# Windowed attention, a gated block and a token and channel mixer on one core: another plan for the first stage, with norms on GpSimd

## The chip, the core and the metric

The kernel runs on one core of one Trainium2 chip. The metric is the device time of one execution in microseconds (us). TensorE (PE in the profile) multiplies matrices into PSUM; VectorE (DVE), ScalarE (ACT) and GpSimd (POOL) work on tiles of 128 partitions; SyncE (SP) issues the DMAs that move data between HBM and SBUF.

## The reference

Three parts follow each other, all in float32 (the weights of the second and third part come as float64 words):

```python
# attention: 4 batches, 8 heads, 576 tokens, head size 64, each token sees itself and 63 before it
scores = where(0 <= rel < 64, q @ k.T / 8, -1e9)
attn = exp(scores - max); attn = attn / (sum(attn) + 1e-9); x = attn @ v
# gated block
h = relu(x @ w_in); u, v = h[..., :512], h[..., 512:]
v_n = (v - mean(v)) / sqrt(var(v) + 1e-6)
x = (u * (w_spatial @ v_n + b_spatial)) @ w_out
# mixer
u = x + (relu(x.T @ w_tok1) @ w_tok2).T
out = u + relu(u @ w_ch1) @ w_ch2
```

## The kernel before

The work up to about 224 us is recorded by a planner, `plan()`; behind it the rest (the product with `w_out`, the mixer) stands in written order and is not touched.

The planner's class `Steps` holds steps with a name, an engine, a rank, a duration, the steps that must be done first and the buffers they take and give back. It plays time forward and records on each engine the possible step that can start first, by rank among equals. The order of each engine's instructions is thereby fixed before the kernel runs; each engine then works its list in order and waits where an input is late.

Attention goes in 18 turns (two passes over batch pairs, nine turns each) of 128 tokens and 8 heads. The steps of turn n, where g is 0 or 1 for a half of four heads:

- `S`: the score products on PE (`scores`), 16 pairs of matmuls into two PSUM banks. For turns below `MASK_PE` = 6 the mask is added on PE too, by one bf16 product of 512 columns for each bank (L278).
- `M`: the row maximum on DVE. For turns below 6 one reduction and one small multiplication (L294, L301); for later ones the mask is added and the maximum found in one custom instruction for each head, from PSUM into the SBUF tile `pb` (L297).
- `X`: four exponentials on ACT with their sums (L306), from PSUM for turns below 6, from `pb` for later ones.
- `N`: on DVE, 1e-9 is added to the sums, the reciprocal taken, and `pb` multiplied by it (L314, L315, L316).
- `T`: four transposes on PE (L488); `C`: the copy of these from PSUM to the tile `PT`, on ACT (L489).
- `V`: the product with the values (L324). The first `PAIRS` = 4 turns have a `V` of their own, later ones go in pairs. `xh`, `xl`: the result split into two rounded parts, on ACT and DVE (L538, L543).

Of these parts come the products of the gated block on PE: `v` (one for each turn, 12 matmuls of 512 columns), then on ACT `R`, on DVE `bn` (L372, L373), on POOL `rs` (L375, L376), on DVE `ts` (L378), and `hi`, `lo`; `u` (four for every third turn, 12 matmuls of 384 columns; evicted by `E`); and `s` (the product over the tokens, 14 matmuls of 288 columns), with `G` on DVE (L406), which multiplies into `U`.

`w_in` is 8 tiles of 512 KB, four for `v` and four for `u`. Each is loaded as float64 words into a piece of `U` and turned into float32 there: `wd` on ACT (into a PSUM bank), `wo` on DVE (two instructions on that bank, L439, L440), `wh` on ACT and `wl` on DVE (L445). `ws` are the tiles of `w_spatial`, split on ACT and DVE. `c2_work` prepares `w_c2` in the same manner in the gaps, with four sums on POOL, and sends it to HBM (`scr`). `wo_work` prepares `w_out`, behind the step `gate`, which waits for the last `xl`; its loads share two buffers (`craw`). SP's first loads stand in one line, in the order in which the tuple before `score` names them.

Of the kernel before, what the change touches and what calls it, by code (L numbers as in the profile page):

```python
# [20 lines left out]
P = 128  # L21
# [4 lines left out]
MASK_PE = 6  # L26
# [3 lines left out]
PAIRS = 4  # L30
# [8 lines left out]
class Steps:  # L39
# [5 lines left out]
    def __init__(self, **room):  # L45
        self.room = {k: [0.0] * n for k, n in room.items()}
        self.clock, self.done, self.open, self.lines = {}, {}, [], {}
        self.pad, self.queue, self.lands = 0, 0.0, [0.0] * 8
# [5 lines left out]
    def start(self, step):  # L54
        name, eng, rank, us, fn, after, take, give, hold, kb = step
        at = self.clock.get(eng, 0.0)
        for a in after:
            if a not in self.done:
                return None
            at = max(at, self.done[a] + self.LAG)  # L60
        for r in set(take):
            free, n = sorted(self.room[r]), take.count(r)
            if len(free) < n:
                return None
            at = max(at, free[n - 1] + self.LAG)
        return max(at, self.lands[-8 + (kb > 520)]) if kb else at

    def run(self):
        while True:
# [10 lines left out]
            gap = at - self.clock.get(eng, 0.0)  # L80
            self.pad = int((gap - 0.5) / 0.3) if PAD and eng == "PE" and gap > 0.8 and at < PAD else 0
# [16 lines left out]
def tile_kernel(ctx, tc, qT, kT, kE, v, w_in, wsT, b_sp, w_out, w_t1, w_t2, w_c1, w_c2, outT):  # L98
# [361 lines left out]
    def plan():  # L460
# [11 lines left out]
        def attend(n):  # L472
# [8 lines left out]
            def turned(g):  # L481
# [7 lines left out]
                copies[n, g] = lambda: nc.scalar.copy(out=PT[0][:, 4 * g:4 * g + 4, :], in_=pt)  # L489

            for g in range(2):
                S.add(("M", n, g), "DVE", 1 + n / 100, 0.95, lambda g=g: smax(n, g), after=[("S", n)], give=free * (n >= MASK_PE))
                S.add(("X", n, g), "ACT", 2 + n / 100, 1.65, lambda g=g: sexp(n, g), after=[("M", n, g)], give=free * (n < MASK_PE), hold=1.54)
                S.add(("N", n, g), "DVE", 1 + n / 100, 1.15, lambda g=g: snorm(n, g), after=[("X", n, g)], hold=1.05)
                S.add(("T", n, g), "PE", 1 + n / 100, 0.65, lambda g=g: turned(g), after=[("N", n, g)], take=free + ["PT"] * (g == 0), give=["pb"] * g, line=("T", n), hold=0.45)
                S.add(("C", n, g), "ACT", 1, 0.6, lambda g=g: copies.pop((n, g))(), after=[("T", n, g)], give=free, hold=0.49)
# [7 lines left out]
        def score(n, after, line):  # L504
            S.add(("S", n), "PE", 0, 1.2 + 0.6 * (n < MASK_PE), lambda: scores(n), after=after + [("Lq", n), "ident"],
                  take=[] if after else ["sp", "sp", "pb"], give=["qk"], hold=1.0 + 0.6 * (n < MASK_PE), line=line)

        def block(ns):
# [36 lines left out]
        def v_work(p, i):  # L545
# [15 lines left out]
            S.add(("v", n), "PE", 10, 2.9, product, after=[("xl", n)] + [("wl", "v", k) for k in range(4)], take=["mm"], hold=2.75, line="work")  # L561
            S.add(("R", n), "ACT", 1.5, 0.6, relu, after=[("v", n)], take=["vf"], give=["mm"], hold=0.49)
            S.add(("bn", n), "DVE", 2, 0.9, part, after=[("R", n)])
            S.add(("rs", n), "POOL", 0, 1.0, part, after=[("bn", n)])
            S.add(("ts", n), "DVE", 2, 0.56, part, after=[("rs", n)])
            S.add(("hi", n), "ACT", 4, 0.6 if i else 2.2, part, after=[("ts", n)])
            S.add(("lo", n), "DVE", 3, 0.7 if i else 1.3, part, after=[("hi", n)], give=["vf"])

        def u_work(p, c, ft):
            g = {}  # L570

            def product():
# [3 lines left out]
            S.add(("u", p, c, ft), "PE", 10, 2.25, product, after=[("xl", 9 * p + 3 * c + k) for k in range(3)] + [("wl", "u", ft)],  # L576
                  take=["mm"], give=["XT"] * (ft == 3), hold=2.09, line="work")
            S.add(("E", p, c, ft), "ACT", 1.5, 0.5 if c == 2 else 0.72, lambda: uv_u_out(p, c, ft, g["ps"]), after=[("u", p, c, ft)], give=["mm"])

        def s_work(b, d, c0):  # L580
# [8 lines left out]
            S.add(("s", b, d, c0), "PE", 10, 2.0, product, after=tiles + [("ws", k, c0) for k in range(6)], take=["mm"], hold=1.86, line="work")  # L589
            S.add(("G", b, d, c0), "DVE", 0.5, 0.47, lambda: spatial_out(b, d, c0, g["ps"]),  # L590
                  after=[("s", b, d, c0)] + [("E", p, c, d) for c in range(2 + b % 2)], give=["mm"], hold=0.4)

        def w_load(kind, k):
            it = (wv_part if kind == "v" else wu_part)(k)
# [3 lines left out]

            S.add(("wL", kind, k), "SP", 0, 0, part, hold=0.47, kb=512, line="SP")
            S.add(("wd", kind, k), "ACT", 1.8 if kind == "v" else 2.5, 0.7, part, after=[("wL", kind, k)], take=["mm"], hold=0.6)  # L600
            S.add(("wo", kind, k), "DVE", 0.8 if kind == "v" else 2.5, 1.25, part, after=[("wd", kind, k)])
            S.add(("wh", kind, k), "ACT", 1.8 if kind == "v" else 2.5, 0.6, part, after=[("wo", kind, k)], hold=0.49)
            S.add(("wl", kind, k), "DVE", 0.8 if kind == "v" else 2.5, 0.7, part, after=[("wh", kind, k)], give=["mm"], hold=0.6)

        def ws_load(k, c):
# [8 lines left out]
            S.add(("wh", k, c), "ACT", 3, 0.45, part, after=[("Lw", k, c)], hold=0.35)  # L614
            S.add(("ws", k, c), "DVE", 2.5, 0.45, part, after=[("wh", k, c)], give=["raw"], hold=0.38)
# [41 lines left out]
        def c2_work(j):  # L657

            rank = 6 + j
# [51 lines left out]
        for fn, *a in ((load_queries, 0), (w_load, "v", 0), (load_queries, 1), (w_load, "v", 1), (load_values, 0), (w_load, "v", 2), (w_load, "v", 3),  # L711
                       (load_queries, 2), (load_values, 1), (w_load, "u", 0), (load_queries, 3), (w_load, "u", 1), (w_load, "u", 2), (w_load, "u", 3)):
# [597 lines left out]
```

## Time and profile before

| | us |
|---|---|
| median of 3 runs (620.10 to 621.08) | 620.14 |
| the profiled execution | 621.39 |
| its span, first to last instruction | 619.5 |
| PE busy in the span | 600.2 (97%) |
| DVE busy | 472.6 (76%) |
| ACT busy | 352.7 (57%) |
| POOL busy | 114.7 (19%) |

The profiled execution is 1.25 us longer than the median, of which 1.9 us lie outside its span. PE's waits sum to some 16 us over the whole span; about 11 us of the first 50 show PE without work. The rows are stretches of a timeline (start, duration, engine, line, operation, tiles, count, and in brackets the idle time before and what ended it), groups of instructions, and busy time in windows.

### The profile page before, as it was taken

What the parts mean: (1) busy time and instruction counts of PE and PEld (TensorE: products, weight loads), DVE (VectorE), ACT (ScalarE), POOL (GpSimd) and SP (SyncE); (2) the same over time, 40 slices, a digit from 0 to 9 for tenths busy, and PEclk for the clock granted to TensorE, in tenths of its full rate; (3) what the DMA queues carried; (4) which work ended last, traced back from release to release, by engine and by line L of the source; (5) the groups of instructions that cost most, each with busy time, mean ns of one, the idle gap of its engine ahead of it and who ended that gap; (6) DMA issues with size and microseconds to landing.
All of it is one profiled execution on the core that took longest, in us unless ns stands there. A gap on an engine that the chain in (4) does not pass through costs nothing.

```text
span 619.5 us, 12149 instructions
## 1 busy us (share of the span) xinstructions
PE 600.2 (97%) x4396; PEld 560.6 (90%) x4396; DVE 472.6 (76%) x1066; ACT 352.7 (57%) x889; POOL 114.7 (19%) x145
## 2 busy tenths in 40 slices
PE   4999999999999989999999999999999999999997
PEld 2678899889988989788988999999999999999997
DVE  5998878968888836586278778888875989866982
ACT  5996786766777532674344454546443557544540
POOL 3000202302422200041025212140011140011320
PEclk8899999999999999999999999999999999999999
DMA  8956356866565652415200524665534674444752
GB/s 325 342 187 188 124 198 228 262 225 223 203 203 180 229 179 69 137 57 167 84 34 35 170 69 169 221 224 168 184 126 173 230 234 159 153 137 170 237 197 77
DMA packets 49812, 108.05 MB, mean 174 GB/s; under 512 B 4948, under 2 KB 17496, under 8 KB 49752
## 3 DMA queue, kind: packets, MB, share of 16 engines
q1 hardware_dynamic: 49752, 107.27, 51.2%
q8 instruction: 35, 0.57, 0.4%
q14 instruction: 25, 0.20, 0.1%
HBM read 86.81 MB, written 20.45 MB: 173 GB/s over the span
## 4 chain that ended last, share of the span: by engine, by line
PE 62%; DVE 4%; DMA 4%; ACT 2%; issue 1%; POOL 0%; ACTq 0%
PE A L1167 19%; PE mm L183 13%; PE mm L955 12%; PE A L955 9%; PE A L183 6%; DMA scr<-raw 3%; PE A L873 1%; DMA craw<-in_w_out 1%; PE A L1251 1%; DVE pb L297 1%; DVE raw L689 0%; ACT raw L686 0%; DVE pb L316 0%; DVE st L372 0%; DVE hid L949 0%
## 5 line engine op out<-in xcount | busy, mean ns | idle before, releaser
L1167 PE MATMUL A<-room,w 128*128 128x384 f32 x720 | 131.1, 335 | 0.7 <-DVE U L1203 0.7
L1167 PEld LDWEIGHTS A<-room,w 128*128 128x128 f32 x720 | 125.1, 188 | 2.1 <-DVE U L1203 1.0
L1161 ACT CAST room<-hid 128x384 fp32r<-128x384 f32 x120 | 61.3, 513 | 48.9 <-PE A L1167 37.5
L1162 DVE TENSOR_TENSOR room<-hid,room 128x384 fp32r<-128x384 f32 x120 | 71.9, 625 | 13.9 <-ACT room L1161 12.2
L949 POOL TENSOR_TENSOR hid<-hid 128x384 f32<-128x384 f32 x36 | 44.2, 1239 | 202.8 <-DVE hid L949 160.0
L183 PE MATMUL mm<-ws,room 128*128 128x288 f32 x416 | 61.0, 297 | 1.6 <-DVE U L406 1.5
L183 PEld LDWEIGHTS mm<-ws,room 128*128 128x128 f32 x416 | 56.7, 188 | 2.6 <-DVE U L406 2.1
L980 ACT ACTIVATE hid<-hid 128x384 f32<-128x384 f32 x54 | 28.1, 525 | 42.4 <-DVE hid L983 42.4
L983 DVE TENSOR_TENSOR hid<-A,hid 128x384 f32<-128x384 f32 x54 | 29.5, 554 | 24.7 <-PE A L955 18.4
L306 ACT ACTIVATE pb<-pb,nm 128x128 f32<-128x128 f32 x96 | 37.2, 392 | 2.8 <-DVE nm L297 2.8
L955 PE MATMUL mm<-room,sh 128*128 128x384 f32 x144 | 37.2, 334 | 0.0
L183 PE MATMUL mm<-xh,wi_h 128*128 128x384 f32 x96 | 33.2, 346 | 0.0
L183 PE MATMUL mm<-xh,wi_l 128*128 128x384 f32 x96 | 32.2, 336 | 0.0
L183 PE MATMUL mm<-xl,wi_h 128*128 128x384 f32 x96 | 32.2, 335 | 0.0
L1192 DVE TENSOR_TENSOR U<-A,U 128x384 f32<-128x384 f32 x42 | 21.9, 551 | 11.1 <-PE A L1167 6.5
L183 PE MATMUL mm<-gh,wo_h 128*128 128x512 f32 (+1 forms) x80 | 30.2, 378 | 0.0
L183 PE MATMUL mm<-gl,wo_h 128*128 128x512 f32 (+1 forms) x80 | 29.6, 370 | 0.2 <-DVE gl L855 0.2
L813 POOL TENSOR_TENSOR k<-k 128x256 f32<-128x256 f32 x12 | 9.7, 832 | 107.1 <-ACT gh L854 59.4
L183 PE MATMUL mm<-gh,wo_l 128*128 128x512 f32 (+1 forms) x80 | 29.5, 369 | 0.0
L855 DVE TENSOR_TENSOR gl<-U,gh 128x512 fp32r<-128x512 f32 (+1 forms) x20 | 13.3, 667 | 21.1 <-ACT gh L854 21.0
L488 PE MATMUL sp<-ident,pb 128*128 128x128 f32 x144 | 21.7, 284 | 7.0 <-DVE pb L316 3.0
L170 ACT CAST sh<-k 128x1024 fp32r<-128x1024 f32 x18 | 18.9, 1050 | 15.7 <-PE mm L955 5.9
(181 smaller groups left out, 1546.0 us busy)
## 6 DMA issues: line engine op xcount, KB each, us to landing
w<-scr SPq DMA_DIRECT2D x63, 512.0 KB, 4.1
scr<-raw SPq DMA_DIRECT2D x48, 256.0 KB, 3.5
k<-sums SPq DMA_DIRECT2D x18, 512.0 KB, 3.8
kk<-in_kT SPq DMA_DIRECT2D x16, 384.0 KB, 5.5
craw<-in_w_c SPq DMA_DIRECT2D x24, 256.0 KB, 3.7
qq<-in_qT SPq DMA_DIRECT2D x18, 256.0 KB, 5.5
va<-in_v SPq DMA_DIRECT2D x18, 256.0 KB, 4.4
vb<-in_v SPq DMA_DIRECT2D x18, 256.0 KB, 4.6
```

Of the source, the lines that this page charges most:

```text
L170: nc.scalar.copy(out=hi, in_=x)
L183: nc.tensor.matmul(o, a, c, start=(i == 0), stop=(i == n - 1))
L306: nc.scalar.activation(out=pb[:, h, :], in_=scs[g][:, h - 4 * g, :] if mk is None else pb[:, h, :], func=AF.Exp, scale=SCALE if mk is None ...
L488: nc.tensor.transpose(pt[:, h, :], pb[:, 4 * g + h, :], ident)
L949: eng.tensor_tensor(out=out, in0=a, in1=b, op=ALU.subtract)
L955: nc.tensor.matmul(o, a, m, start=first and i == 0, stop=i == len(todo) - 1, skip_group_check=True)
L980: nc.scalar.activation(out=o, in_=src, func=AF.Relu)
L983: nc.vector.tensor_tensor(out=o, in0=a, in1=b, op=ALU.add)
L1161: nc.scalar.copy(out=oh, in_=blk[j])
L1162: nc.vector.tensor_tensor(out=ol, in0=blk[j], in1=f(oh), op=ALU.subtract)
L1167: nc.tensor.matmul(acc[d], a, m, start=(first and j == 0 and i == 0), stop=(last and j == NJ - 1 and i == 2), skip_group_check=True)
L1192: nc.vector.tensor_tensor(out=at, in0=src, in1=at, op=ALU.add)
```

## The change

The planner gets new numbers: a table of ranks, a table `SLACK` of extra time that it adds behind inputs by the kind of step, a cost for PE's change from one kind of product to another, and new durations. Beside that:

- `MASK_PE` = 0: no mask on PE; all turns use the custom instruction on DVE and take their exponentials from `pb`. The score banks come free behind `M` then.
- The norm is cut in two steps: `I` (the sum's addition and the reciprocal, on DVE) and `N` (the multiplication), which for the turns in `EARLY`, 0 to 9, is on POOL.
- `C` is on DVE for turns 4 to 8.
- `PAIRS` = 6: six turns have a `V` of their own.
- The `u` tiles 0, 2 and 3 of `w_in` are formed in SBUF in their own words (`wu_pool`), without a PSUM bank, and their `wl` is on POOL.
- The first loads stand in another order (`ORDER`).

The diff, cut to its core:

```diff
-MASK_PE = 6
+MASK_PE = 0
-PAIRS = 4
+PAIRS = 6
+EARLY = range(0, 10)
+CD0 = range(4, 9)
+CD1 = range(4, 9)
+PU = (0, 2, 3)
+ORDER = (0, 1, 4, 2, 7, 9, 3, 6, 5, 10, 12, 8, 11, 13)
+RANK = dict(M=3.84, X=22.11, I=-0.06, N=5.51, T=3.58, C=-0.53, ...)
+SLACK = dict(cd=0.68, cs=0, ch=3.08, cl=0.65, oh=1.62, ol=0.52, ...)
...
+        lag = self.LAG + SLACK.get(name[0], 0.0)
         for a in after:
...
-                at = max(at, self.done[a] + self.LAG)
+                at = max(at, self.done[a] + lag)
...
-        nc.vector.tensor_tensor(out=pb[:, hs, :], in0=pb[:, hs, :], in1=rs.unsqueeze(2).to_broadcast([P, w, 128]), op=ALU.mult)
+        yield
+        eng = nc.gpsimd if n in EARLY else nc.vector
+        eng.tensor_tensor(out=pb[:, hs, :], in0=pb[:, hs, :], in1=rs.unsqueeze(2).to_broadcast([P, w, 128]), op=ALU.mult)
...
+    def wu_pool(ft):
+        fs = slice(128 * ft, 128 * ft + 128)
+        raw = U[:, ft, :1024]
+        words = raw.rearrange("p (a c w) -> p a c w", a=4, w=2)
+        x, y, low = words[:, :, :, 1], words.bitcast(I32)[:, :, :, 1], words.bitcast(I32)[:, :, :, 0]
+        hi, lo = wi_h[:, :, fs], wi_l[:, :, fs]
+        nc.sync.dma_start(...)
+        yield
+        down(x, y)
+        yield
+        nc.vector.tensor_scalar(out=y, in0=y, scalar1=3, scalar2=None, op0=ALU.logical_shift_left)
+        nc.vector.scalar_tensor_tensor(out=y, in0=low, scalar=29, in1=y, op0=ALU.logical_shift_right, op1=ALU.bitwise_or)
+        yield
+        nc.scalar.copy(out=hi, in_=x)
+        yield
+        nc.gpsimd.tensor_tensor(out=lo, in0=x, in1=f(hi), op=ALU.subtract)
...
+                    if n in (CD0, CD1)[g]:
+                        nc.vector.tensor_copy(out=out, in_=pt)
+                    else:
+                        nc.scalar.copy(out=out, in_=pt)
```

What the planner makes of it is seen in the lists of the engines. The first place is DVE's list from the end of the first `v` tiles to the first `xl`, before:

```order
L314 TENSOR_SCALAR rs<-sm 128x4
L315 RECIPROCAL rs<-rs 128x4
L316 TENSOR_TENSOR pb<-pb,rs 128x512
L445 TENSOR_TENSOR wi_l<-mm,wi_h 128x512
L439 TENSOR_SCALAR mm<-mm 128x512
L440 SCALAR_TENSOR_TENSOR mm<-U,mm 128x512
L439 TENSOR_SCALAR mm<-mm 128x512
L440 SCALAR_TENSOR_TENSOR mm<-U,mm 128x512
L445 TENSOR_TENSOR wi_l<-mm,wi_h 128x512
L294 TENSOR_REDUCE mx<-sc 128x4
L301 TENSOR_SCALAR nm<-mx 128x4
L543 TENSOR_TENSOR xl<-xo,xh 128x4x128
```

and now, around the first `xl` (L328 and L329 are `I`, L474 and L475 `wo` in SBUF, L455 and L456 `wo` in PSUM, L588 `xl`, L461 `wl`):

```order
L328 TENSOR_SCALAR rs<-sm 128x4
L329 RECIPROCAL rs<-rs 128x4
L474 TENSOR_SCALAR U<-U 128x512
L475 SCALAR_TENSOR_TENSOR U<-U 128x512
L328 TENSOR_SCALAR rs<-sm 128x4
L329 RECIPROCAL rs<-rs 128x4
L455 TENSOR_SCALAR mm<-mm 128x512
L456 SCALAR_TENSOR_TENSOR mm<-U,mm 128x512
L588 TENSOR_TENSOR xl<-xo,xh 128x4x128
L455 TENSOR_SCALAR mm<-mm 128x512
L456 SCALAR_TENSOR_TENSOR mm<-U,mm 128x512
L461 TENSOR_TENSOR wi_l<-mm,wi_h 128x512
```

The large multiplication behind each pair of small instructions is gone from DVE, and `xl` of turn 0 now stands ahead of the `wo` of two of the four `v` tiles, where before it stood behind all four.

The second place is POOL's list behind its set-up. Before, it holds only the two small instructions of `rs` for each `v` product:

```order
L375 TENSOR_SCALAR rstd<-mv 128x1
L376 TENSOR_TENSOR rstd<-rstd,mhalf 128x1
```

and now the multiplications of the norms (L332), the low parts of the three `u` tiles (L479) and `rs` (L391, L392) stand in one line:

```order
L479 TENSOR_TENSOR wi_l<-U,wi_h 128x4x128
L332 TENSOR_TENSOR pb<-pb,rs 128x512 x2
L479 TENSOR_TENSOR wi_l<-U,wi_h 128x4x128
L332 TENSOR_TENSOR pb<-pb,rs 128x512
L479 TENSOR_TENSOR wi_l<-U,wi_h 128x4x128
L391 TENSOR_SCALAR rstd<-mv 128x1
L392 TENSOR_TENSOR rstd<-rstd,mhalf 128x1
L332 TENSOR_TENSOR pb<-pb,rs 128x512
```

Twenty multiplications came to POOL, with the waits of the norms now between those of `rs`.

The third place is SP's list at the end of the plan, where `w_out` is loaded (`craw<-in_w_out`) and the first loads of the mixer's weights begin (`in_w_t`), before:

```order
L621 DMA craw<-in_w_out 128x512 x3
L692 DMA scr<-raw 128x512
L621 DMA craw<-in_w_out 128x512
L692 DMA scr<-raw 128x512 x2
L784 DMA k_3418<-in_w_t 128x2x512
L784 DMA k_3420<-in_w_t 128x2x512
L621 DMA craw<-in_w_out 128x512
L784 DMA k_3422<-in_w_t 64x512
L692 DMA scr<-raw 128x512
L621 DMA craw<-in_w_out 128x512
```

and now:

```order
L670 DMA craw<-in_w_out 128x512 x2
L741 DMA scr<-raw 128x512
L670 DMA craw<-in_w_out 128x512 x2
L741 DMA scr<-raw 128x512 x3
L670 DMA craw<-in_w_out 128x512 x2
L741 DMA scr<-raw 128x512 x2
L670 DMA craw<-in_w_out 128x512 x2
L834 DMA k_3415<-in_w_t 128x2x512
L834 DMA k_3417<-in_w_t 128x2x512
```

The last two loads of `w_out` stood behind loads of the mixer; now all eight stand ahead of them.

## Rows read from the trace of the kernel before

**Rows 1.** Windows: us, then busy time (instructions) of each engine, clock, DMA, GB/s

```profile
10.00:20.00 10.00, 6.62 (x66) 4.80 (x70) 9.72 (x21) 7.84 (x25) 0.00 (x0) 0.53 1.04 391
...
40.00:50.00 10.00, 9.03 (x53) 7.80 (x53) 9.66 (x24) 9.36 (x31) 2.04 (x4) 1.00 0.23 68
```

**Rows 2.** Timeline of PE: scores, `V`, `u`, `v` and transposes

```profile
5.05 1.99 PE L283 MATMUL sc<-kk,qq 64*64 64x128 f32 x32
...
8.68 1.10 PE L283 MATMUL sc<-kk,qq 64*64 64x128 f32 x32 [0.98 <-DMA kk<-in_kT]
...
20.75 1.24 PE L183 MATMUL mm<-wi_h,xh 128*128 128x512 f32 x4
...
53.28 0.34 PE L324 MATMUL mm<-PT,va 128*64 128x64 f32 x4
...
54.36 1.98 PE L283 MATMUL sc<-kk,qq 64*64 64x128 f32 x64
56.27 0.45 PE L183 MATMUL mm<-xh,wi_h 128*128 128x384 f32 x1
...
58.49 1.08 PE L183 MATMUL mm<-wi_h,xh 128*128 128x512 f32 x4
...
61.45 0.63 PE L488 MATMUL sp<-ident,pb 128*128 128x128 f32 x4
61.83 1.18 PE L183 MATMUL mm<-wi_h,xh 128*128 128x512 f32 x4
```

**Rows 3.** DMA of the first 60 us: GB/s in 40 slices of 1.5 us

```profile
GB/s 0 184 416 298 368 412 411 322 403 412 396 404 393 377 382 402 403 398 391 98 103 213 347 276 229 264 164 254 96 0 0 98 0 0 99 81 337 220 260 339
```

**Rows 4.** Timeline of DVE in the first 57 us: norms, weights, statistics, masks

```profile
10.01 0.16 DVE L314 TENSOR_SCALAR rs<-sm 128x4 f32<-128x4 f32 x1
10.21 0.18 DVE L315 RECIPROCAL rs<-rs 128x4 f32<-128x4 f32 x1
10.42 0.69 DVE L316 TENSOR_TENSOR pb<-pb,rs 128x512 f32<-128x512 f32 x1
11.03 0.68 DVE L445 TENSOR_TENSOR wi_l<-mm,wi_h 128x512 fp32r<-128x512 f32 x1
11.63 0.69 DVE L439 TENSOR_SCALAR mm<-mm 128x512 int32<-128x512 int32 x1
...
12.96 0.16 DVE L314 TENSOR_SCALAR rs<-sm 128x4 f32<-128x4 f32 x1
...
28.97 0.69 DVE L372 BATCH_NORM_STATS2 st<-vf 128x6 f32<-128x512 f32 x1
29.69 0.18 DVE L373 BATCH_NORM_AGGREGATE mv<-st 128x2 f32<-128x6 f32 x1
29.79 0.67 DVE L439 TENSOR_SCALAR mm<-mm 128x512 int32<-128x512 int32 x1
...
50.30 1.19 DVE L167 TENSOR_TENSOR ws<-raw,ws 128x288 fp32r<-128x288 f32 x3
...
55.71 0.28 DVE L297 CUSTOM_DVE_ANT_0 pb<-sc,msk 128x128 f32<-128x128 f32 x1
...
56.55 0.29 DVE L297 CUSTOM_DVE_ANT_0 pb<-sc,msk 128x128 f32<-128x128 f32 x1
```

**Rows 5.** POOL's largest group by line: busy us, mean ns, idle time before

```profile
L949 POOL TENSOR_TENSOR hid<-hid 128x384 f32<-128x384 f32 x36 | 44.2, 1239 | 202.8 <-DVE hid L949 160.0 <-DVE room L1162 24.8 <-ACT sh L170 11.9
```

**Rows 6.** One line of DVE, L689: ns min/median/max, first and last start

```profile
L689 DVE TENSOR_TENSOR raw<-cx,raw x24: 415/420/959, 89.5 to 209.0; 128x256 fp32r<-128x256 f32 x24
```

**Rows 7.** Timeline of POOL and DVE at 160 us

```profile
160.49 0.92 POOL L679 TENSOR_TENSOR cy<-cx 128x256 f32<-128x256 f32 x1
160.84 0.85 DVE L378 TENSOR_SCALAR vf<-vf,mv,rstd 128x512 f32<-128x512 f32 x1
```

**Rows 8.** A piece of the chain that ended last: start, us, what

```profile
215.39 7.40 DMA craw<-in_w_out
```

**Rows 9.** Timeline of ACT and PE at the end of the plan

```profile
220.56 0.43 ACT L136 ACTIVATE val<-craw 128x256 f32<-128x256 f32 x1 [4.58 <-DMA craw<-in_w_out]
...
222.19 1.98 PE L183 MATMUL mm<-ws,room 128*128 128x288 f32 x13 [1.48 <-DVE U L406]
```

More of the change, by code (lines that the diff above doesn't have):

```diff
@@ L505, in score @@
             S.add(("S", n), "PE", 0, 1.2 + 0.6 * (n < MASK_PE), lambda: scores(n), after=after + [("Lq", n), "ident"],
-                  take=[] if after else ["sp", "sp", "pb"], give=["qk"], hold=1.0 + 0.6 * (n < MASK_PE), line=line)
+                  take=[] if after else ["sp", "sp", "pb"], give=["qk"], hold=0.98 + 0.6 * (n < MASK_PE), line=line)
         def block(ns):
@@ L530, in block @@
             for m in ns:
-                S.add(("xh", m), "ACT", 0, 0.6, lambda m=m: xhigh(m), after=[("V", m)], hold=0.49)
-                S.add(("xl", m), "DVE", 0, 0.7, lambda m=m: xlow(m), after=[("xh", m)], give=["mm" if m > n else "xo"], hold=0.6)
+                S.add(("xh", m), "ACT", RANK["xh"], 0.6, lambda m=m: xhigh(m), after=[("V", m)], hold=0.49)
+                S.add(("xl", m), "DVE", RANK["xl"], 0.7, lambda m=m: xlow(m), after=[("xh", m)], give=["mm" if m > n else "xo"], hold=0.6)
         def xhigh(n):
@@ L574, in product @@
                 uv_u_mm(p, c, ft, g["ps"])
-            S.add(("u", p, c, ft), "PE", 10, 2.25, product, after=[("xl", 9 * p + 3 * c + k) for k in range(3)] + [("wl", "u", ft)],
-                  take=["mm"], give=["XT"] * (ft == 3), hold=2.09, line="work")
-            S.add(("E", p, c, ft), "ACT", 1.5, 0.5 if c == 2 else 0.72, lambda: uv_u_out(p, c, ft, g["ps"]), after=[("u", p, c, ft)], give=["mm"])
+            S.add(("u", p, c, ft), "PE", 10, 2.3, product, after=[("xl", 9 * p + 3 * c + k) for k in range(3)] + [("wl", "u", ft)],
+                  take=["mm"], give=["XT"] * (ft == 3), hold=2.17, line="work")
+            S.add(("E", p, c, ft), "ACT", RANK["E"], 0.5 if c == 2 else 0.72, lambda: uv_u_out(p, c, ft, g["ps"]), after=[("u", p, c, ft)], give=["mm"])
         def s_work(b, d, c0):
@@ L588, in s_work @@
             tiles = [("lo", 9 * p)] + [("lo", 9 * p + 1 + 4 * (b % 2) + m) for m in range(4)]
-            S.add(("s", b, d, c0), "PE", 10, 2.0, product, after=tiles + [("ws", k, c0) for k in range(6)], take=["mm"], hold=1.86, line="work")
-            S.add(("G", b, d, c0), "DVE", 0.5, 0.47, lambda: spatial_out(b, d, c0, g["ps"]),
+            S.add(("s", b, d, c0), "PE", 10, 2.05, product, after=tiles + [("ws", k, c0) for k in range(6)], take=["mm"], hold=1.93, line="work")
+            S.add(("G", b, d, c0), "DVE", RANK["G"], 0.47, lambda: spatial_out(b, d, c0, g["ps"]),
                   after=[("s", b, d, c0)] + [("E", p, c, d) for c in range(2 + b % 2)], give=["mm"], hold=0.4)
         def w_load(kind, k):
-            it = (wv_part if kind == "v" else wu_part)(k)
+            pool_does = kind == "u" and k in PU
+            it = (wv_part if kind == "v" else wu_pool if pool_does else wu_part)(k)
             def part():
                 next(it, 0)
+            bank_of = [] if pool_does else ["mm"]
+            a, d = RANK["a" + kind], RANK["d" + kind]
+            eng = "POOL" if pool_does else "DVE"
             S.add(("wL", kind, k), "SP", 0, 0, part, hold=0.47, kb=512, line="SP")
[L600 to L603, printed above, removed]
+            S.add(("wd", kind, k), "ACT", a, 0.75, part, after=[("wL", kind, k)], take=bank_of, hold=0.6)
+            S.add(("wo", kind, k), "DVE", d, 1.25, part, after=[("wd", kind, k)])
+            S.add(("wh", kind, k), "ACT", a, 0.6, part, after=[("wo", kind, k)], hold=0.49)
+            S.add(("wl", kind, k), eng, d, 1.5 if pool_does else 0.7, part, after=[("wh", kind, k)], give=bank_of, hold=1.4 if pool_does else 0.6)
         def ws_load(k, c):
@@ L613, in ws_load @@
             S.add(("Lw", k, c), "SP", 60, 0, part, take=["raw"], hold=0.5 + 0.5 * (k > 3), kb=150, line="SP")
-            S.add(("wh", k, c), "ACT", 3, 0.45, part, after=[("Lw", k, c)], hold=0.35)
-            S.add(("ws", k, c), "DVE", 2.5, 0.45, part, after=[("wh", k, c)], give=["raw"], hold=0.38)
+            S.add(("aw", k, c), "ACT", RANK["aw"], 0.45, part, after=[("Lw", k, c)], hold=0.35)
+            S.add(("ws", k, c), "DVE", RANK["dw"], 0.45, part, after=[("aw", k, c)], give=["raw"], hold=0.38)
         def fetch_words(name, src, after, rank, line):
```

49 lines of the change are left out of this document (32 added, 17 removed).

## The prediction

> **What bounds the kernel now.** I read the busy times by window first. PE is the busiest engine by far, and behind the first 50 us it hardly pauses; so time is to be had only from the ramp at the start and from the few waits behind it. In the ramp the engine that never rests is DVE: 9.72 of 10 us in the second window and 9.66 in the fifth, with the two between alike [rows 1]. PE in the second window works 6.62 us, at a granted clock of 0.53, half of full speed, which is the lower of its two levels, 1.2 of 2.4 GHz [rows 1]. The timeline of PE shows that level: 16 pairs of score products take 1.99 us at 5.05, and the same 1.10 us at 8.68 [rows 2].
>
> The ramp is over when PE has a store of `v` and `u` products to draw on. As its mark I take the start of PE's first `u` product of tile 3 of `w_in`: in the kernel before at 56.27 us, with eight `S`, twelve half turns of `T`, six `V`, three `v` and three `u` behind it [rows 2]. In the changed list of PE the same set stands ahead of the place just behind the sixth `V`. So the ramp is compared at an equal amount of work, and whatever this point comes earlier is gained if nothing later takes it back. PE's prices at the full clock, from start to start: `V` 1.08 us (53.28 to 54.36), `S` 0.96 (two in 1.91), `u` 2.22 (56.27 to 58.49), `v` 2.96 (58.49 to 61.45), half a `T` 0.38 (61.45 to 61.83) [rows 2].
>
> The second place is the end of the plan. The chain that ended last goes through a load of `w_out` that took 7.40 us [rows 8]. ACT waited 4.58 us for another one of these loads, DVE's list stood behind, and PE waited 1.48 us for `G` [rows 9].
>
> **The change, part by part.** *DVE's work up to the mark.* The sixth `V` needs both `C` of turn 5, which are now on DVE, so I sum DVE's list up to the second of them. Prices from start to start [rows 4]: half an `M` 0.84 us (four heads, 55.71 to 56.55); `wo` 1.33 (11.63 to 12.96); `wl` 0.60 (11.03 to 11.63), and `xl`, `C`, `lo` and `ts` of 512 columns the same; `bn` 0.82 (28.97 to 29.79); `ws` 0.40 (three in 1.19). The multiplication that leaves DVE costs 0.61 (10.42 to 11.03). What stays of the norm, `I`, took 0.41 (10.01 to 10.42) with the dependent multiplication behind it. An independent instruction can start 0.10 us after a small one (29.69 to 29.79), so `I` is 0.20 + 0.10 = 0.30, with 0.20 and 0.41 as its bounds.
>
> PE's first scores start when their keys are there, at about 5.05 as before, and DVE's first two `M` halves behind them end at about 8.7 (5.05 + 1.99, then twice 0.84). Then DVE must wait for the second scores. Their keys now stand behind 512 KB more (the values of turn 0). They landed just before 8.68 [rows 2]; at some 400 GB/s [rows 3] this is 1.3 us later, 9.8 to 10. The clock is low then, since PE has paused for almost 3 us, so the scores take 1.99 us and DVE goes on at 11.75. From there to the second `C` of turn 5 its list holds twelve half `M` (10.1), twelve `I` (3.6), seven `wo` (9.3), five `wl` and five `xl` (6.0), three `bn` (2.5), three `ts` and three `lo` (3.6), four `C` (2.4) and six `ws` (2.4): 39.9 us. Two short waits, for the third scores and the second `v` tile, add 0.8 by the same rate of the DMAs. DVE is there at 52.4, the sixth `V` runs from 52.5 to 53.6. That is 2.7 us ahead of 56.27.
>
> *PE's own path to the mark.* DVE's list reaches the last `wl` of the `v` tiles at about 27.3, so the first `v` starts near 27.5, later than the 20.75 of before [rows 2]; the loads of the `v` tiles come later too. Behind it stand three `v` (8.9), six half `T` (2.3), four `V` (4.3), three `S` (2.9) and three `u` (6.7): 25.1 us, to 52.6 with the sixth `V` included. This is 1 us less than DVE needs: DVE binds, and PE's side has little to spare. If the first `v` still runs at the low clock, with the ratio 1.99 to 1.10 it costs 2.4 us more, of which 1 is covered.
>
> *The mask products.* Twelve bf16 products leave PE. They stood in the ramp, where DVE sets the end, so I give them nothing of their own. The cover is DVE's list; were DVE quicker they would count. The exponentials take slightly longer from `pb`, on ACT, which has its ten copies of turns 4 to 8 taken away; nothing added on the path.
>
> *The multiplications on POOL.* Price: 384 columns took 1.24 us [rows 5]; for 512 columns this bounds it from below, and in proportion it is 1.65. I take 1.3 to 1.5, since a part of the 1.24 does not grow with the columns. For each half turn `T` comes 0.7 to 0.9 us later behind `I` than on DVE, which the other turns in flight cover. On POOL's list the low parts of three `u` tiles stand between; they are needed 15 us later.
>
> *What POOL takes back from DVE.* No row shows POOL multiplying through the ramp. But rows show both engines slowed where they meet: at 160 us a DVE instruction that does what I price at 0.60 takes 0.85 beside a POOL operation of 0.92 [rows 7], and of 24 equal DVE instructions with two inputs in SBUF, 420 ns in the middle, one took 959 [rows 6]. So a meeting costs up to 0.54. Up to the mark DVE has fifteen such instructions behind 11.75: three `wo` in SBUF, six `ws`, three `ts`, three `lo`. POOL is busy about half of that time (some twelve multiplications and two low parts), and a meeting falls on average in the middle of the other's: a quarter of 0.54, 15 × 0.135 = 2.0 us. Bounds 0 and 8.1. The nearest row to my value is the 0.25 excess of the 0.85, at half of the instructions. The mark then comes at 55.6: the ramp gives **0.7 us**.
>
> The Trainium skill, "SBUF — State Buffer", section "Who interferes with whom", states that VectorE with two SBUF inputs and GpSimd share a port pair, and that the loser of its lock is blocked for the other's whole instruction. The rows at 160 us agree in direction. By that rule alone each of the fifteen could pay up to a whole POOL operation; this is the third case below, which is priced from the rows.
>
> *The end of the plan.* All loads of `w_out` now stand ahead of the mixer's 512 KB loads, and PE's list has three `v` instead of two between the last `V` and the last `u`. Either covers the 1.48 us of PE's wait [rows 9]. I count **1.5 us**, with 0 as the other bound. What is late next there is nothing that the trace shows.
>
> *Single turns and `SLACK`.* Turns 4 and 5 as singles order `S` ahead of `V`; costs no instruction. The extra time in the plan moves readers back from writers; I give it nothing, and it is part of the spread.
>
> Sum: 0.7 + 1.5 = 2.2 us. The profiled execution would fall from 621.39 to 619.2 (span 619.5 to 617.3); the median of the runs is 1.25 below the profiled one, so 620.14 − 2.2 = **617.9**.
>
> **The rivals.** *First, POOL costs DVE nothing.* Then 2.7 + 1.5 = 4.2: **615.9**. For it: most of the 24 instructions in [rows 6] ran at their 420 ns. If besides `I` is 0.20 each (1.2 us less in all) and the second keys are no later than before (1.3), it is 613.4. Against it: [rows 7].
>
> *Second, the end of the plan gives nothing*, since a PE that comes earlier finds the loads as late as before; the chain through them [rows 8] hangs on the last `xl`, which moves with PE, and that speaks against it. 620.14 − 0.7 = **619.4**, within measurement of no change.
>
> *Third, slower: DVE is held by POOL.* Every one of the fifteen meets an operation and pays the 0.54 that the row shows at most. The mark comes 8.1 us later than with free ports, 5.4 later than before; less 1.5 at the end, **624.0**. The point from which it is slower than 620.14 by more than can be told (1.2 us): 2.7 + 1.5 + 1.2 = 5.4 us, 0.36 for each of the fifteen; at 0.43 each it is 622.4. For it speaks that DVE's list up to the mark has no slack, since DVE binds; against it that POOL itself also waits, and that it pauses between turns.
>
> **How the numbers follow.** My forecast, 617.9 with 616.6 to 619.2 around it, gets 0.40; ports free 0.26; the end without gain 0.16; DVE held 0.18. What differs by less than 0.2%, 1.24 us, cannot be told from no change here. Faster takes the forecast but for its upper edge, all of the first rival and a small part of the second: 0.60. Same: the rest of the forecast, the second and a little of the third: 0.23. Slower: 0.17. The range goes from 613.4, the first rival with the cheap bounds, to 622.4, the third at 0.43: some 0.1 is left out on each side.
>
> **What would show it.** Right: DVE unbroken from about 11.8 to beyond 50 us; the first `v` on PE at 27 to 29; the sixth `V` ending at 53.6 to 57; no wait of PE for `G` near the end of the plan. POOL's multiplication at 1.3 to 1.5 us, and `ws`, `ts`, `lo` by some 0.1 to 0.3 longer in the ramp. Wrong: the sixth `V` ending later than 57; PE waiting between 60 and 200 us for `pb` from POOL; the granted clock low beyond 30 us; the last `w_out` load as late as before against PE.

## The result, and the profile of the changed kernel

| | before | after |
|---|---|---|
| median of four runs, us | 620.45 | 616.02 |
| lowest and highest | 620.10, 621.08 | 615.31, 616.45 |
| ratio of the two, with its 95% interval | 1 | 0.9918 (0.9903 to 0.9933) |
| span of the profiled execution, us | 619.5 | 613.5 |

By the two medians the kernel became 4.4 us faster; by the recorded ratio, which is not the ratio of these medians, it is 5.1 (4.2 to 6.0); 2.2 were forecast. One execution of either kernel can lie a microsecond from its median, and the two profiled ones lie on opposite sides, so their spans differ by 6.0 us. The places of the gain are read from this pair; how much the change is worth is read from the ratio.

Three points with the same products of PE behind them in both kernels (but for the mask products) divide the 6.0 us: the prediction's mark, the start of the last row of `s` products that no other product interrupts, and the first product with `w_out`. The last two are these, before and then after:

```profile
209.43 1.87 PE L183 MATMUL mm<-ws,room 128*128 128x288 f32 x13
241.27 0.40 PE L183 MATMUL mm<-gh,wo_h 128*128 128x512 f32 x1
```
```profile
205.59 1.87 PE L197 MATMUL mm<-ws,room 128*128 128x288 f32 x13
235.28 0.40 PE L197 MATMUL mm<-gh,wo_h 128*128 128x512 f32 x1
```

| stretch of PE's list | before | after | gain |
|---|---|---|---|
| start to the mark | 56.27 | 55.33 | 0.94 |
| mark to the last row of `s` | 153.16 (to 209.43) | 150.26 (to 205.59) | 2.90 |
| from there to the first `w_out` product | 31.84 (to 241.27) | 29.69 (to 235.28) | 2.15 |
| the rest | 378.23 | 378.22 | 0.01 |

The first row is the ramp, forecast at 0.7. The third is the end of the plan, forecast at 1.5. The second was forecast at nothing.

The windows show where PE stands still. Columns: window, its length, then busy time and instructions of PE, PE's weight loads, DVE, ACT and POOL, granted clock, DMA share, GB/s. The changed kernel:

```profile
10.00:20.00 10.00, 8.71 (x112) 6.91 (x112) 7.32 (x45) 8.59 (x38) 4.21 (x4) 1.00 1.05 404
20.00:30.00 10.00, 6.38 (x106) 5.33 (x106) 9.37 (x31) 10.00 (x31) 3.65 (x4) 0.85 1.06 389
30.00:40.00 10.00, 10.00 (x102) 8.23 (x101) 9.83 (x51) 9.57 (x31) 5.75 (x7) 0.98 0.58 190
40.00:50.00 10.00, 10.00 (x130) 8.90 (x130) 9.55 (x37) 9.95 (x39) 5.56 (x8) 1.00 0.56 165
...
200.00:230.00 30.00, 30.00 (x219) 30.00 (x218) 16.56 (x39) 10.87 (x24) 0.66 (x1) 1.00 0.50 163
```

Against [rows 1], DVE still works almost all the time from 20 to 50 us, and now PE does too: it works without a pause from 25.81 us to beyond 230 (the empty list of waits below covers what the windows leave out). In the kernel before, PE's waits between 56 and 232 us were these (line, what it waited for, us in total, times, longest):

```profile
PE sp L488 <- DVE pb L316: 1.5, 2, 1.3
PE mm L183 <- DVE U L406: 1.5, 1, 1.5
PE sp L488 <- DVE rs L314: 0.5, 1, 0.5
```

The same view of the changed kernel is empty. The waits for `pb` and `rs` make 2.0 us of the second stretch. PE also drains ahead of a wait: each of the three groups of four transposes there took 0.60 us instead of 0.38 from start to start, 0.7 together. A pause of 0.14 us at 182.22, too short for this view, costs some 0.3 with its draining. Together these make the 2.90. The wait for `U`, 1.48 us, is the main part of the third stretch [rows 9]; from start to start PE lost 1.64 with it, and 0.52 more with a second short wait for `U`, at 224.45.

PE's list in the ramp (start, duration, engine, line, operation, tiles, count, idle time before and what ended it):

```profile
10.87 1.98 PE L297 MATMUL sc<-kk,qq 64*64 64x128 f32 x32 [3.79 <-DMA kk<-in_kT]
...
24.33 0.40 PE L297 MATMUL sc<-kk,qq 64*64 64x128 f32 x2 [1.24 <-DMA kk<-in_kT]
25.81 1.10 PE L297 MATMUL sc<-kk,qq 64*64 64x128 f32 x30 [1.08 <-ACT PT L529]
...
29.45 1.59 PE L197 MATMUL mm<-wi_h,xh 128*128 128x512 f32 x4
...
55.33 0.66 PE L522 MATMUL sp<-ident,pb 128*128 128x128 f32 x4
```

In the ramp PE waits 12.9 us in all, each time ahead of 26 us and mostly for queries and keys; from 25.81 it never stops. Waits are left only in those first 26 us, where the DMAs bring 404 and 389 GB/s (windows from 10 to 30 us).

DVE in the same stretch:

```profile
13.00 0.29 DVE L311 CUSTOM_DVE_ANT_0 pb<-sc,msk 128x128 f32<-128x128 f32 x1 [2.36 <-PE sc L297]
...
18.53 1.41 DVE L475 SCALAR_TENSOR_TENSOR U<-U 128x512 int32<-128x512 int32 x1
...
28.58 0.69 DVE L475 SCALAR_TENSOR_TENSOR U<-U 128x512 int32<-128x512 int32 x1
...
41.61 1.70 DVE L394 TENSOR_SCALAR vf<-vf,mv,rstd 128x512 f32<-128x512 f32 x2
...
53.52 0.68 DVE L527 COPY PT<-sp 128x512 f32<-128x512 f32 x1
```

and POOL beside two of these rows:

```profile
18.30 1.08 POOL L332 TENSOR_TENSOR pb<-pb,rs 128x512 f32<-128x512 f32 x1 [1.18 <-DVE rs L329]
...
23.82 1.29 POOL L479 TENSOR_TENSOR wi_l<-U,wi_h 128x512 fp32r<-128x512 f32 x1 [2.40 <-ACT wi_h L477]
...
41.84 1.19 POOL L332 TENSOR_TENSOR pb<-pb,rs 128x512 f32<-128x512 f32 x1 [0.18 <-DVE rs L329]
```

The `wo` at 18.53 started 0.23 us behind a multiplication of POOL and took 1.41 us; the next one met no work of POOL and took 0.69.

At the end of the plan the last two loads of `w_out` (`craw`) now stand ahead of the mixer's (`in_w_t`), and ACT's last wait for one is 1.25 us; one of those before was 4.58 [rows 9]:

```profile
206.25 1.53 SPq L670 DMA_DIRECT2D craw<-in_w_out  x2
208.04 4.39 SPq L834 DMA_DIRECT2D k<-in_w_t  x8
```
```profile
210.53 0.43 ACT L150 ACTIVATE val<-craw 128x256 f32<-128x256 f32 x1 [1.25 <-DMA craw<-in_w_out]
```

### The profile page after: what moved, and what is told of

The parts are those of the page before. It is cut to its first block, busy times and chain, and to the rows that moved or that the text cites. A ratio compares the mean times of both kernels' runs of the same rounds, so it can differ in the third digit from the quotient of the medians.

```text
span 613.5 us, 12232 instructions
## 1 busy us (share of the span) xinstructions
PE 596.1 (97%) x4384; PEld 561.6 (92%) x4384; DVE 465.4 (76%) x1125; ACT 347.7 (57%) x879; POOL 138.9 (23%) x168
## 4 chain that ended last, share of the span: by engine, by line
PE 93%; ACT 3%; DVE 2%; DMA 1%; issue 0%; SPq 0%; ACTq 0%; DVEq 0%
PE mm L197 36%; PE A L1217 20%; PE mm L1005 12%; PE A L1005 9%; PE A L197 6%; PE sc L297 3%; PE sp L522 2%; PE xo L340 2%; PE A L923 1%; DMA kk<-in_kT 1%; PE mm L340 1%; ACT pb L320 1%; PE A L1301 1%; ACT PT L529 0%; DVE hid L999 0%
## 5 line engine op out<-in xcount | busy, mean ns | idle before, releaser
L320 ACT ACTIVATE pb<-pb,nm 128x128 f32<-128x128 f32 x144 | 56.0, 395 | 4.1 <-DVE nm L311 4.1
L311 DVE CUSTOM_DVE_ANT_0 pb<-sc,msk 128x128 f32<-128x128 f32 x144 | 32.2, 283 | 13.6 <-PE sc L297 13.4
L297 PE MATMUL sc<-kk,qq 64*64 64x128 f32 x576 | 22.0, 298 | 12.5 <-DMA kk<-in_kE 5.1
L297 PEld LDWEIGHTS sc<-kk,qq 64*64 64x64 f32 x576 | 18.2, 147 | 14.4 <-issue 10.7
L332 POOL TENSOR_TENSOR pb<-pb,rs 128x512 f32<-128x512 f32 x20 | 21.6, 1079 | 38.0 <-DVE rs L329 21.5
```

The lines of the kernel that those rows point to most:

```text
L297: nc.tensor.matmul(scs[e][64 * q:64 * q + 64, j, :], qq[er, j, 64 * q:64 * q + 64], kk[er, j, step * q:step * q + 128], start=not on_pe, s ...
L311: nc.vector.tensor_tensor_reduce(out=pb[:, 4 * g + h, :], in0=scs[g][:, h, :], in1=mk, scale=-SCALE, scalar=3e38, op0=ALU.add, op1=ALU.min ...
L320: nc.scalar.activation(out=pb[:, h, :], in_=scs[g][:, h - 4 * g, :] if mk is None else pb[:, h, :], func=AF.Exp, scale=SCALE if mk is None ...
```

## Experiments

Each ratio is against runs of the kernel before on the same chip; the changed kernel stands at 0.9918 (0.9903 to 0.9933). A thousandth is 0.62 us. In the runs of the changed kernel the mark is read as the start of the next product behind the sixth `V`, 55.33 us without an edit.

### Does VectorE set the ramp?

The norms' multiplications go back to VectorE, and every list keeps its order:

```diff
-        eng = nc.gpsimd if n in EARLY else nc.vector
+        eng = nc.vector
```

> The changed kernel with its order of steps untouched, but the twenty multiplications of the norms issued on VectorE where the plan put them for GpSimd. Theory: DVE's list sets the ramp. Up to the mark (behind the sixth V) it takes up about 13 multiplications of 0.61 us, 7.9 us, and saves the 1.4 us that its own instructions lost beside GpSimd, so the mark comes some 6 us later than 55.3 (61 to 62) and the time is 621 to 623. Rival: the loads and PE set the ramp and DVE has slack; then the mark stays at 55 to 57 and the time at 616 to 618.

Measured: 1.0007 (0.9990 to 1.0024), 5.5 us slower than the changed kernel. The mark stood at 61.58 us, 6.2 later; 1.1 of these had built up when the scores began that start at 25.81 in the changed kernel (26.90). The windows show PE with holes and DVE without:

```profile
40.00:50.00 10.00, 9.26 (x105) 7.85 (x104) 9.79 (x45) 9.98 (x38) 2.62 (x5) 1.00 0.55 155
50.00:60.00 10.00, 7.84 (x97) 6.90 (x98) 9.82 (x29) 7.08 (x28) 1.14 (x2) 1.00 0.39 119
```

So work added to DVE comes through to the end nearly whole. That an order of its own would help was tried too, with `EARLY = ()` and the plan made anew:

> The changed kernel with all norms on VectorE, planned anew (EARLY empty). Theory: DVE has some 13 multiplications of 0.61 us more up to the mark, 8 us, and no order hides that, less the 1 us that it loses beside GpSimd; mark at 60 to 62, 621 to 625. Rival: with its own order the planner covers them, as in the kernel before; 617 to 618.

Measured: 1.0194 (1.0180 to 1.0209), worse than with the order untouched. PE waits once for 7.23 us:

```profile
42.53 1.09 PE L522 MATMUL sp<-ident,pb 128*128 128x128 f32 x4 [7.23 <-DVE pb L332]
```

The move of the norms is needed. A plan made anew with another set of steps mixes two effects, the step's and the order's; the single moves below are therefore taken back with the order kept.

### What did GpSimd cost VectorE?

```diff
-        eng.tensor_tensor(out=pb[:, hs, :], ...)
+        if n not in EARLY:
+            eng.tensor_tensor(out=pb[:, hs, :], ...)
```

> The changed kernel without the twenty multiplications of the norms on GpSimd (the rows of turns 0 to 9 are not divided by their sums), all lists else the same. Theory: DVE is the bound of the ramp and lost 1.4 us beside GpSimd (one wo of 1.41 instead of 0.69 us, two ts of 1.70 instead of 1.1 us); without the multiplications the mark comes 0.7 to 1.4 us earlier, at 54 to 54.5, and the time is 614.5 to 615.3. Rival: PE's own list, unbroken from 25.8 us, is the bound; mark at 55.2, time as the changed kernel, 616. If GpSimd had held DVE for more than its rows show, the time would be under 614.

Measured: 0.9913 (0.9894 to 0.9932), by its time not to be told from the changed kernel. The trace tells more. The same two places on DVE:

```profile
18.56 0.69 DVE L476 SCALAR_TENSOR_TENSOR U<-U 128x512 int32<-128x512 int32 x1
...
41.42 0.97 DVE L395 TENSOR_SCALAR vf<-vf,mv,rstd 128x512 f32<-128x512 f32 x2
```

0.69 instead of 1.41, and 0.97 instead of 1.70: the two meetings cost DVE 1.45 us, and the other instructions that I had counted took the same in both kernels to some hundredths. The mark came 1.1 us earlier (54.23), the last row of `s` began 0.8 earlier (204.80), and the span is 0.8 shorter (612.7). That the 1.45 us came through to these points is not shown, for PE's granted clock differs between the two executions as well. Here it was 1.00:

```profile
28.00:30.00 2.00, 2.00 (x12) 1.72 (x12) 1.93 (x10) 1.97 (x8) 0.00 (x0) 1.00 1.07 405
```

In the changed kernel it was 0.50 (last section), and the second `V`, four transposes and the first four products of `v` took PE 4.04 us there (26.84 to 30.88) and 2.50 here (26.82 to 29.32). By the other executions both seem to be needed for a gain. Where the mean granted clock was below 0.999, this kernel's spans were 613.7 to 615.2 us, like the changed kernel's 613.5 to 614.3. At 0.999 and 1.00 they were 612.3 to 612.8, but the changed kernel's one execution at 1.00 had 614.6. That rests on six executions of one kernel and four of the other, and the ratio does not show it.

### Would the second keys help?

Two neighbours of the first loads change places on SP, the queries and keys of turn 1 and the values of turn 0; all other lists stay:

```diff
-  S.add(("Lq", n), ..., lambda: load_qk(n), ...)
+  S.add(("Lq", n), ..., lambda: load_v(0) if n == 1 else load_qk(n), ...)
-  S.add(("Lv", n), ..., lambda: load_v(n), ...)
+  S.add(("Lv", n), ..., lambda: load_qk(1) if n == 0 else load_v(n), ...)
```

> The changed kernel with two neighbours of the first loads exchanged: the queries and keys of turn 1 ahead of the values of turn 0; every engine's list but SP's stays word for word. Theory: DVE, which waited 2.36 us for the second scores and is the bound from there on, goes on 1.3 us earlier; mark at 54, the time 1.3 us under that of the changed kernel, about 614.7. Rival: the loads behind hold PE anyway (it waited for keys of turn 4 at 24.3 us); mark at 55 to 55.5 and no change against the changed kernel.

Measured: 0.9915 (0.9900 to 0.9931), no change; the mark stood at 55.26 us (55.33 in the changed kernel). The second scores did start 0.9 us earlier, and the gain was gone at the next ones:

```profile
9.94 1.98 PE L297 MATMUL sc<-kk,qq 64*64 64x128 f32 x32 [2.88 <-DMA kk<-in_kT]
14.26 2.10 PE L297 MATMUL sc<-kk,qq 64*64 64x128 f32 x32 [1.09 <-DMA kk<-in_kT]
...
24.43 0.40 PE L297 MATMUL sc<-kk,qq 64*64 64x128 f32 x2 [1.68 <-DMA kk<-in_kT]
```

My theory fell here: DVE is not the bound from 12 us on. Up to about 24 us PE waits mostly for loads, and an exchange among them only moved the wait. That faster loads would move the mark, no run shows.

### The mask and the copies

The changed kernel in its own order, with the mask of turns 0 to 5 on PE again:

```diff
-        on_pe = n < MASK_PE
+        on_pe = n < 6
```

> The changed kernel in its own order, but turns 0 to 5 take the mask on PE by 12 bf16 products, and maximum and exponentials from PSUM. Theory: PE and DVE end together at the mark, so the 12 products (0.27 us each at the full clock, 3 to 4 us with the first ones at the low clock) come on top where PE is unbroken, behind 25.8 us: six of them, 1.6 us, and banks that come free behind the exponentials add to it; 617.5 to 620. Rival: DVE alone is the bound, and its maximum by one reduction and a small multiplication is 0.1 us shorter for each half turn; 614.8 to 616.

Measured: 0.9961 (0.9948 to 0.9975), 2.7 us slower than the changed kernel; the mark stood at 58.12 us, 2.8 later. Mask products waited twice, by their place in the list for a bank that was not yet free (the profile puts the second wait down to a `wo`, which ended 0.02 us behind the last exponentials):

```profile
15.77 0.59 PE L292 MATMUL sc<-msk,ident 128*128 128x512 bf16 x1 [1.11 <-ACT pb L320]
...
26.98 1.06 PE L292 MATMUL sc<-msk,ident 128*128 128x512 bf16 x2 [1.72 <-DVE mm L455]
```

So taking the mask off PE is worth something in this list, though it makes DVE's work longer. How much of the 2.7 us is PE's added work and how much the later banks, the run does not separate.

Then the ten copies of turns 4 to 8 back on ScalarE:

```diff
-                    if n in (CD0, CD1)[g]:
+                    if False:
```

> The changed kernel in its own order, with the ten copies of turns 4 to 8 issued on ScalarE. Up to the mark DVE has four copies of 0.60 us less, ACT four of 0.47 more. Theory: ACT is as full there (9.6 to 9.95 of every 10 us from 20 to 60 us), so the mark stays or comes up to 1.5 us later; 616 to 618. Rival: DVE alone binds; mark up to 2 us earlier, 614 to 615.

Measured: 0.9942 (0.9928 to 0.9956), 1.5 us slower, though the interval overlaps the changed kernel's a little. ACT has become the engine without a pause, and DVE has gaps:

```profile
50.00:60.00 10.00, 8.65 (x125) 7.85 (x122) 8.24 (x32) 10.00 (x39) 2.88 (x3) 1.00 0.67 219
```

In this profiled execution the second keys also came 1.3 us later than in the changed kernel's, so its mark (57.34) is not a clean measure; the ratio is. PE, DVE and ACT are about equally full ahead of the mark (9.55 us or more of every 10 from 40 to 60 us in the changed kernel), and each of the three runs that put work back on one of them was slower. The six single turns, the `u` tiles in SBUF and the order of the first loads were not taken back one by one.

### What took away the waits in the middle?

The whole table of extra time taken out of the changed kernel:

```diff
-SLACK = dict(cd=0.68, cs=0, ch=3.08, ...)
+SLACK = {}
```

> The changed kernel with every entry of SLACK taken away, planned anew. Theory: the extra time that the planner leaves behind inputs took away PE's waits between the mark and the last products of s; without it they come back, 2 to 3 us between 56 and 206 us, and perhaps the wait for G of 1.5 us; 618 to 620. Rival: those waits went because DVE has less to do; then no change, 615.5 to 616.8, with no wait of PE over 0.3 us behind 56 us.

Measured: 1.0116 (1.0093 to 1.0139), 12.3 us slower than the changed kernel, far beyond what I expected. The mark came only 1.8 us later (57.11), though with one `u` product of 2.2 us fewer ahead of it, so most of the loss lies behind it. To separate the two, the table was counted only for inputs ready before 60 us of the planner's time:

```diff
-                at = max(at, self.done[a] + lag)
+                at = max(at, self.done[a] + (lag if self.done[a] < 60 else self.LAG))
```

> The changed kernel with SLACK counted only where the input is done before 60 us of the planner's time; PE's list is the same up to about 80 us. Theory: the slack keeps PE's waits away in the middle; the mark stays at 55.2, but behind it waits of 3 to 8 us return for transposes, 619 to 625. Rival: the loss of the kernel without slack came from its ramp; mark at 55.2, no waits, 616 to 617.

Measured: 1.0117 (1.0091 to 1.0143), the same loss. The mark stood at 55.38 us, as in the changed kernel, and PE's waits between 56 and 218 us, where the changed kernel has none, are:

```profile
PE sp L522 <- DVE pb L332: 4.5, 4, 1.9
PE sp L522 <- POOL pb L332: 1.3, 3, 0.6
PE sp L522 <- ACT PT L529: 1.0, 1, 1.0
PE sp L522 <- ACT pb L320: 0.8, 1, 0.8
PE mm L197 <- DVE U L422: 0.7, 1, 0.7
PE sp L522 <- ACT raw L735: 0.3, 1, 0.3
```

8.6 us of waits, mostly of transposes for a norm. The span of this execution is 14.0 us longer than the changed kernel's. Of the other 5.4 us, 0.8 is one more wait near the end, and some 2.4 would be PE's draining, 0.2 us for each of the twelve. Some 1.6 is the granted clock, which stood at 0.50 for 3.4 us behind the longest of the waits (from 156.60) and was 1.00 there in the changed kernel: four transposes and eight products of `v` took 3.91 us (156.54 to 160.45), where the changed kernel's take 0.38 and 1.93 at the full clock (the eight from 58.27 to 60.20). The rest is not traced.

```profile
158.00:160.00 2.00, 2.00 (x7) 1.52 (x6) 1.95 (x7) 0.37 (x1) 0.00 (x0) 0.50 0.35 135
```

Behind the mark the changed kernel is fast because its planner keeps readers away from writers.

Is the table worth the same in the kernel before? First all of it, planned anew:

> The kernel before with the table SLACK alone, planned anew. Theory: the three waits of PE for the norms behind the mark (1.33, 0.50, 0.17 us and what the drained engine loses with them) go, the ramp stays as it was (mark at 56 to 57); 617.5 to 618.5, or 616 if the wait for G goes too. Rival: the table does nothing by itself; 620 to 621.

Measured: 1.0021 (1.0005 to 1.0037), slightly slower. PE's wait for `G` was gone, but in the ramp PE now waited 4.3 us for the low parts of the `v` tiles. With the ramp's order left alone (the table counted only behind 60 us):

> The kernel before with the table SLACK counted only where the input is done behind 60 us of the planner's time; the ramp's order is that of the kernel before. Theory: the slack alone takes away PE's waits behind the mark (2.0 us, and some 0.7 for the engine that drains with each); the mark stays at 56 to 57; 617.5 to 618.7, or 616.5 with the wait for G gone too. Rival: it needs the new ranks and moves beside it, and puts other waits in their place; 620 or more.

Measured: 0.9984 (0.9971 to 0.9997), about 1.0 us faster. The mark, as the prediction reads it, stood where it did before (56.43 and 56.27), and of PE's 3.5 us of waits from 56 to 232 us 1.2 are left:

```profile
PE mm L185 <- DVE U L408: 0.6, 1, 0.6
PE sp L490 <- DVE pb L318: 0.5, 1, 0.5
```

The direction is the theory's; the size is under what it expected. At last the reverse, the planner's numbers without any move between engines (mask, norms, copies, `u` tiles, single turns and loads as before):

> The changed kernel with its planner's numbers (RANK, SLACK, SWITCH, durations), but the mask on PE for six turns, all norms on VectorE, all copies on ScalarE, four single turns, all u tiles through PSUM and the first loads in the old order. Theory: the numbers carry the middle and the end of the plan, the moves between engines only the ramp, 0.9 us; 616.5 to 617.5 with the mark at 56 to 58. Rival: the numbers are worth nothing without the moves, since DVE is then as full as before; 620 or more.

Measured: 1.0108 (1.0084 to 1.0132). The theory fell: the numbers alone make the kernel slower, by waits in the ramp, 6.2 us for `rs` and 3.4 us for `pb` among them. Numbers and moves belong together.

### The loads at the end

In the kernel before, the mixer's first load is held back by one small instruction on VectorE into its tile, so that all loads of `w_out` stand ahead of it:

```diff
             raw = k4().bitcast(I32)
+            if not raws and parts[0][0].shape[-1] == 256:
+                nc.vector.memset(raw[:, :1], 0)
```

> The kernel before with one small instruction on VectorE that holds back the mixer's first load (one column of its tile is set first), so that all eight loads of w_out stand ahead of it on SP; else as before. Theory: the last loads of w_out land 3 to 5 us earlier and PE's wait of 1.48 us for G goes; 618.9 to 619.2 where the kernel before takes 620.4. Rival: the wait moves on, to the mixer's first product or to another input of DVE; 620 to 621.

Measured: 0.9977 (0.9964 to 0.9989), 1.4 us faster, as expected. SP's list and ACT's last wait:

```profile
214.81 0.33 SPq L621 DMA_DIRECT2D craw<-in_w_out  x1
226.73 4.17 SPq L786 DMA_DIRECT2D k<-in_w_t  x8
```
```profile
218.68 0.43 ACT L136 ACTIVATE val<-craw 128x256 f32<-128x256 f32 x1 [2.31 <-DMA craw<-in_w_out]
```

PE's wait for `G` is gone, and the mixer, whose loads begin 15 us later than before, does not miss them.

## Why the prediction was right, and where it was not

**The sign, the range and the two named places hold.** 616.0 lies in the range from 613.4 to 622.4, and both terms of the sum, ramp and end, came about near their sizes: 0.9 for 0.7, and 2.15 in the stretch that holds the 1.48 us, for 1.5. The gain as a whole is twice the forecast, because of a third place. The time is that of the first rival, 615.9, but not for its reason: the ports were not free.

**The ramp's sum, step by step.** The second scores let DVE go on at 13.00 us instead of 11.75. They took 1.98 us as forecast, but not because the clock had fallen in the pause ahead of them: no rise was on record before 16.70 (last section). From there to the end of the second `C` of turn 5 at 54.2 its list took 41.2 us; 39.9 for the work, 0.8 for waits and 2.0 for POOL make 42.7. The two errors cancelled, and the mark came at 55.33 for a forecast of 55.6: that closeness is luck. The list was shorter partly because a `wo` in SBUF takes 1.07 us (28.12 to 29.19), not the 1.33 of one in PSUM. The 2.0 for POOL was 1.45, but not by fifteen small losses: two meetings lost 0.7 each, eight of the fifteen ran beside no instruction of POOL, and the other five lost 0.05 at most. The most that I had read from [rows 6], 0.54, was too low for one meeting; the number of meetings was far too high. The third rival, in which each of the fifteen pays, fell with that.

The Trainium skill, "SBUF — State Buffer", section "Who interferes with whom", says that the blocked engine waits for the other's whole instruction. The trace comes near that for the `wo` at 18.53 us: it lost 0.72 us, and POOL's multiplication of 1.08 had 0.85 still to run.

**"DVE binds" was half of the truth.** Behind 26 us it holds: 13 more multiplications on DVE put the mark 6.2 us later, 5.2 of them lost behind that point. But PE, which I had 1 us ahead of DVE, had nothing in hand: its first `v` came at 29.45 instead of 27.5, and from 25.81 on its list has no gap at all. A part of that is the granted clock, 0.50 from about 27 to 30.4 us: it cost PE some 1.5 us on the second `V`, the transposes and the first quarter of the first `v`. The prediction had named a first `v` at the low clock as a condition, and a low clock beyond 30 us as a sign of being wrong; that sign was just touched. Ahead of 26 us PE's waits are mostly for loads, and exchanging two of these moved a wait and not the mark. And work that I priced at nothing because DVE covers it is not free: the mask back on PE costs 2.7 us, the copies back on ACT 1.5.

**POOL's price failed as a bound.** I took 1.24 us for 384 columns [rows 5] as a lower bound for 512 columns and forecast 1.3 to 1.5; the multiplication takes 1.04. The 1.24 is a mean of two kinds. Nine of the 36 took 1.01 to 1.02 us and the others 1.20 to 1.39, and all of the longer ones began while DVE ran a `TENSOR_TENSOR`, of the nine only four; so the price probably held meetings already. And the row was of an operation with two full inputs; `wl` on POOL, also of two, takes 1.29 with 512 columns, while the multiplication reads one full input and a broadcast one. A mean, and a row of another form, was no bound.

**The step that failed is the last term, "The extra time in the plan moves readers back from writers; I give it nothing".** It is the 2.9 us of the second stretch. The rows were there: I had counted the waits behind 50 us as "few" and spoke of the last only, though the other three held 2.0 us, and every one of them was a transpose that stood too close behind its norm, which is what `SLACK` acts on. Without the table behind 60 us the changed kernel loses 12.3 us. On the kernel before the table behind 60 us is worth about 1.0 us in all, the end of the plan included, so the 2.9 come from the table together with the new order, and how they divide between the two the runs do not settle.

## What to carry to other kernels

When a planner that orders in-order engines gets new numbers, price them by the waits that they can remove: list every wait of the bounding engine, however small, by the distance between its writer and its reader. Here a plan without extra time between them lost 12.3 us to late inputs, and the planner's numbers made the kernel slower with another set of steps; so test a move with the order held, and the order apart from the moves. A lower bound from another instruction form, or from a mean that already holds delays, is no bound. And before two traces are compared at a mark, compare their granted clocks.

## What the runs showed of the hardware

A DVE instruction that began while a multiplication of POOL ran lost a part of what was left of it, and for the large ones most of it. Against the kernel without the multiplications, the `ws` at 40.38 us lost 0.05 with 0.16 left, the `wo` at 18.53 lost 0.72 with 0.85 left, the second `ts` (42.05) 0.72 with 0.98 left, and behind the mark a `ws` at 56.06 lost 0.31 with 0.45 left. The counted instructions that began first (at 18.08, 39.22 and 41.61) lost nothing, and the multiplications that they met took 1.08, 1.08 and 1.19 us instead of 1.04.

The windows print a granted clock of 1.00 for the start of a trace, but the trace's list of clock levels begins only at its first entry, at 7.24 us in the kernel before and at 16.70 in the changed one; ahead of it nothing is recorded. How fast PE was there is read from its products. In twelve of the fourteen traces the second scores lie ahead of the first entry and take 1.98 or 1.99 us; in the kernel before and its run with the mixer held back they lie behind it, at a recorded 1.00, and take 1.10. So 1.99 us at 5.05 [rows 2] fits the lower level, as the prediction read it, although the window of that trace prints 1.00 there:

```profile
4.00:6.00 2.00, 1.95 (x22) 1.08 (x25) 0.00 (x0) 0.00 (x0) 1.59 (x5) 1.00 0.91 328
```

The same holds for the 1.98 us of the second scores in the changed kernel. Behind its first entry the clock of the changed kernel falls once, after three windows of 2 us with 0.70, 1.09 and 0.59 us of PE's work:

```profile
20.00:22.00 2.00, 0.70 (x22) 0.63 (x25) 1.55 (x5) 2.00 (x5) 1.04 (x1) 1.00 1.05 391
22.00:24.00 2.00, 1.09 (x24) 0.68 (x15) 1.97 (x5) 2.00 (x7) 0.18 (x1) 1.00 1.05 379
24.00:26.00 2.00, 0.59 (x10) 0.38 (x14) 1.94 (x4) 2.00 (x10) 1.11 (x1) 1.00 1.07 379
26.00:28.00 2.00, 2.00 (x52) 1.83 (x49) 1.99 (x11) 2.00 (x8) 1.04 (x1) 0.74 1.08 408
28.00:30.00 2.00, 2.00 (x20) 1.82 (x18) 1.93 (x10) 2.00 (x8) 0.27 (x1) 0.50 1.04 389
30.00:32.00 2.00, 2.00 (x9) 1.64 (x8) 2.00 (x14) 2.00 (x6) 2.00 (x2) 0.91 0.91 300
```

There the second `V` takes 1.85 us instead of 1.08.
